# Second layer of a fused attention and MoE kernel as seven products of quarters, with single buffers that make room for it

## Chip, cores, metric

One core of one Trainium2 chip. The metric is the device time of one execution in microseconds. The kernel before takes 723.83 us (median of 3 runs, 723.74 to 724.42).

## The reference, cut

A gated linear attention (4 batches, 8 heads, 768 steps, 48 per head) feeds a two-layer block on 3072 tokens:

```python
def _moe_ref(x, w_in, w_out):      # x 3072x384, w_in 384x2048, w_out 2048x384, all float32
    h = x @ w_in
    g = h * np.cos(h)
    return (g @ w_out).astype(np.float32)
```

The tokens come in 12 groups of 2 x 128 rows; the attention of a group is computed in chunks of 128 steps. The second layer, `g @ w_out`, is what the change rewrites.

## The kernel before: the parts that matter

```python
    def load(g, names, i=None):                       # inputs of group g, on the SP queue
        ...                                           # v has two buffers, the others one
    def g_phase(g, i):                                # "phs": running sum of phases
        matmul(ps, lhsT=turns, rhs=cut(x["tan"], i, 1), start=True, stop=first)
        if not first:                                 # needs tan of the chunk before
            matmul(ps, lhsT=last, rhs=prev, start=False, stop=True)
        ...                                           # ACT casts, VectorE writes tan
    def f_transpose(g, i, n, name):                   # called for kT, then for qT
        tr = ft.tile([C, NB, n * H, 32], F32, tag="tr", name="tr")   # two buffers
        nc.vector.transpose(out=tr, in_=X[g][name[0] + "s"]...)
        moved = rows_d.tile(...)                      # in DRAM
        nc.sync.dma_start(out=moved..., in_=tr)
        # four DMAs DRAM -> kT, or one DRAM -> qT
    def f_scores(n, hh):                              # "sc": reads kT and qT
    def f_xt(g):                                      # yT -> DRAM ("x") -> xT, on the SP queue
    def mm1(g, jp):                                   # "hp": first layer, 6 matmuls of 256 columns
        gate = msb.tile(..., name="gate", bufs=10)
    def mm2(g, i, j0, nj):                            # "op": second layer, 384 columns
        for j in range(j0, j0 + nj):
            matmul(ps, lhsT=gate..., rhs=w_out[:, j], ...)

    def weave(*parts):      # each part: items, from, to; order of the calls = sorted by position
    ...
    for n in range(2, NG):
        weave((logs(n + 1), 0.0, 0.02), (chunks(n), 0.0, 0.36), (second(n - 1, 0), 0.0, 0.38),
              (prods(n + 1), 0.38, 0.39), (each(g_angle, n + 1), 0.39, 0.4),
              (second(n - 1, 1), 0.4, 0.56), (phases(n + 1), 0.49, 0.51),
              (keys(n + 1), 0.52, 0.7), (first(n), 0.56, 1.0), ...)
```

One pass of this loop is a period of about 55 us. The SP queue issues one transfer after the other, so that one that waits holds up all behind it. The order of issue is that of the built program, and not always that of these calls: group 3's `v` is named after `x` and `xT` of group 1, and yet its first load is issued ahead of `x` in the trace below.

## Time and profile before

In the profile's lines PE is TensorE (matrix products), PEld its weight loads, DVE VectorE, ACT and POOL two further engines, SPq the DMA queue of the sync engine. A record is one instruction in the trace; an f32 matmul leaves two.

| | before |
|---|---|
| median of runs | 723.83 us |
| profiled span, granted TensorE clock | 725.1 us, 0.973 |
| TensorE / VectorE / ACT busy | 95% / 55% / 54% |
| second layer of one group | 64 records, 20.65 us |
| start of the first layer (`hp`) of group 1 | 130.8 us |
| mean of eight steady periods (starts of `hp`, groups 2 to 10) | 55.1 us |

### The profile page before, as it was taken

The page shows a single profiled execution, that of the slowest core. Times are in us where ns is not written, and L with a number is a line of the kernel's source. Part 1 is how long each engine was busy: PE and PEld are TensorE (multiplying, and loading weights), DVE is VectorE, ACT ScalarE, POOL GpSimd, SP SyncE. Part 2 cuts the span into 40 slices and gives each one's busy share as a digit, 9 for nine tenths or more (in the row PEclk, how much of TensorE's full clock was granted, in tenths as well). Part 3 has the DMA queues.
Part 4 walks back from the last instruction along what each step waited for, and adds up shares of the span by engine and source line. Part 5 has one row for each costly group of instructions (what it writes and reads, how often), then busy time and mean ns, then how long its engine had stood idle before and what let it go on. Part 6 is the DMA issues. An engine that isn't in the chain of part 4 may idle for free.

```text
span 725.1 us, 9428 instructions
## 1 busy us (share of the span) xinstructions
PE 689.0 (95%) x3574; PEld 523.1 (72%) x3574; DVE 396.3 (55%) x598; ACT 393.3 (54%) x728; POOL 31.4 (4%) x68
## 2 busy tenths in 40 slices
PE   3499799999999999999999999999999999999995
PEld 3397567886886886876776786786786786786773
DVE  4777998553644654655645645645645645731110
ACT  6667796373473484485475475375376376241330
POOL 2001110000000010010010010010010010000000
PEclk9678899999999999999999999999999999999998
DMA  9926726806626566565575575575575482161000
GB/s 269 253 84 156 192 97 130 199 13 141 158 51 146 150 170 131 153 182 130 149 187 128 145 163 120 140 174 123 141 173 122 131 173 69 58 129 55 12 0 28
DMA packets 232115, 94.74 MB, mean 131 GB/s; under 512 B 208366, under 2 KB 220529, under 8 KB 232060
## 3 DMA queue, kind: packets, MB, share of 16 engines
q1 hardware_dynamic: 225324, 68.55, 42.9%
q0 software_dynamic: 6016, 25.17, 10.1%
q8 instruction: 30, 0.49, 0.3%
q10 hardware_dynamic: 720, 0.33, 0.2%
q14 instruction: 25, 0.20, 0.1%
HBM read 69.22 MB, written 24.81 MB: 130 GB/s over the span
## 4 chain that ended last, share of the span: by engine, by line
PE 85%; DMA 6%; DVE 5%; ACT 1%; issue 1%; SPq 1%; POOL 0%; DVEq 0%
PE op L637 33%; PE hp L637 29%; PE sc L637 6%; PE yp L637 5%; PE sp L637 4%; PE phs L637 4%; DMA qT<-moved 2%; PE lgs L637 2%; DMA end<-row 1%; DVE w_out L606 1%; DVE w_out L603 1%; PE yr L637 1%; PE tp L799 1%; DMA raw<-in_moe_w_in_dram 1%; DMA im<-in_a_im_dram 1%
## 5 line engine op out<-in xcount | busy, mean ns | idle before, releaser
L637 PE MATMUL op<-w_out,gate 128*128 128x384 f32 x768 | 262.6, 489 | 0.9 <-DVE w_out L606 0.9
L637 PE MATMUL hp<-xT,w_in 128*128 128x256 f32 x1152 | 255.2, 383 | 0.6 <-ACT xT L860 0.6
L637 PEld LDWEIGHTS hp<-xT,w_in 128*128 128x128 f32 x1152 | 221.8, 193 | 35.0 <-ACT xT L860 1.0
L637 PEld LDWEIGHTS op<-w_out,gate 128*128 128x128 f32 x768 | 142.3, 190 | 95.0 <-issue 3.7
L904 DVE TENSOR_TENSOR gate<-hp,gate 128x512 f32<-128x512 f32 x96 | 65.6, 684 | 135.3 <-ACT gate L653 135.3
L905 ACT ACTIVATE junk<-hp 128x512 bf16<-128x512 f32 x96 | 57.2, 596 | 84.0 <-DVE gate L904 84.0
L653 ACT ACTIVATE gate<-hp,half_pi_b 128x512 f32<-128x512 f32 x96 | 65.7, 684 | 43.2 <-PE hp L637 43.0
L637 PEld LDWEIGHTS sc<-qT,kT 96*128 96x128 f32 x384 | 49.3, 197 | 9.3 <-issue 2.5
L637 PE MATMUL sc<-qT,kT 96*128 96x128 f32 x384 | 50.9, 283 | 1.3 <-DMA qT<-moved 0.9
L818 DVE TENSOR_TENSOR atm<-sc,causal 128x512 f32<-128x512 f32 x48 | 33.0, 687 | 24.7 <-PE sc L637 24.7
L716 DVE SCALAR_TENSOR_TENSOR mag<-Q,lg 128x768 f32<-128x768 f32 (+1 forms) x13 | 11.6, 895 | 63.5 <-ACT Q L653 63.5
L838 ACT COPY yT<-yp 48x512 f32<-48x512 f32 x44 | 25.4, 578 | 38.6 <-PE yp L637 37.9
L748 ACT CAST tan<-phs 128x384 int32<-128x384 f32 x24 | 11.5, 479 | 63.8 <-PE phs L637 63.8
L918 ACT ACTIVATE ot<-op 128x384 f32<-128x384 f32 x24 | 11.6, 482 | 48.6 <-PE op L637 48.6
L652 ACT ACT_TABLE_LOAD x26 | 33.4, 1283 | 0.5
L637 PE MATMUL yp<-atm,v 128*48 128x128 f32 x352 | 33.5, 277 | 0.0
L637 PE MATMUL sp<-v,ks 128*96 128x48 f32 x320 | 29.6, 245 | 0.0
L637 PE MATMUL yp<-qT,state 96*48 96x128 f32 x304 | 29.6, 272 | 0.0
L637 PEld LDWEIGHTS sp<-v,ks 128*96 128x96 f32 x320 | 29.4, 165 | 0.3 <-issue 0.2
L749 DVE TENSOR_TENSOR tan<-phs,tan 128x384 f32<-128x384 f32 x24 | 13.4, 556 | 27.1 <-ACT tan L748 27.0
L617 ACT ACTIVATE e<-e,least_e_b 128x384 f32<-128x384 uint32 (+1 forms) x28 | 18.3, 655 | 16.1 <-DVE e L615 16.0
L637 PE MATMUL lgs<-lg,sums 128*128 128x384 f32 x48 | 19.3, 523 | 7.7 <-DVE lg L690 7.7
(96 smaller groups left out, 695.4 us busy)
## 6 DMA issues: line engine op xcount, KB each, us to landing
moved<-tr SPq DMA_DIRECT2D x20, 768.0 KB
raw<-in_moe_w_in_dram POOLq DMA_DIRECT2D x24, 512.0 KB, 6.1
raw<-in_moe_w_out_dram POOLq DMA_DIRECT2D x32, 384.0 KB, 4.1
kT<-moved SPq DMA_DIRECT2D x40, 192.0 KB
qT<-moved SPq DMA_DIRECT2D x10, 768.0 KB
re<-in_a_re_dram SPq DMA_DIRECT2D x24, 192.0 KB
im<-in_a_im_dram SPq DMA_DIRECT2D x24, 192.0 KB
k<-in_k_dram SPq DMA_DIRECT2D x24, 192.0 KB
```

The costliest lines, as they stand in the source:

```text
L617: nc.scalar.activation(out=e.bitcast(F32), in_=e, func=AF.Relu, scale=-1.0, bias=least_e_b, accum_out=odd[:, ds(next(odds), 1)])
L637: chain(nc.tensor.matmul(out, **kw), "tensor")
L652: chain(nc.scalar.preload_act_table_set(loaded[0]))
L653: chain(nc.scalar.activation(func=func, **kw))
L716: nc.vector.scalar_tensor_tensor(out=u, in0=Q, scalar=HUGE, in1=P, op0=ALU.min, op1=ALU.mult)
L748: nc.scalar.copy(out=ph.bitcast(I32), in_=ps)
L749: nc.vector.tensor_tensor(out=ph, in0=ps, in1=ph.bitcast(I32), op=ALU.subtract)
L818: nc.vector.tensor_tensor(out=y["atm"][:, ts(hh, HH)], in0=ps, in1=causal.unsqueeze(1).to_broadcast([C, HH, C]), op=ALU.mult)
L838: nc.scalar.copy(out=X[g]["yT"][half, :, i], in_=ps[half])
L904: nc.vector.tensor_tensor(out=gate, in0=ps, in1=gate, op=ALU.mult)
L905: nc.scalar.activation(out=junk, in_=ps, func=AF.Square, scale=1.0 / in_scale, accum_out=wide[:, ds(g * (NJ // 2) + jp, 1)])
L918: nc.scalar.mul(out=ot, in_=ps, mul=1.0 / (in_scale * out_scale))
```

## The change

Intent: multiply the 256 x 2048 gates by the 2048 x 384 `w_out` in 2 x 2 quarters with seven products instead of eight (Strassen's method in the form with 15 sums). TensorE does an eighth less in the second layer of 11 groups; VectorE adds the quarters. The sums need room, which is found in buffers.

```diff
-                                     bufs=2 if name == "v" else 1)
+                                     bufs=1)
-    RAW = 6
+    RAW = 4
-        low = stage.tile([C, n], U32, tag="low", name="low")
+        low = stage.tile([C, n], U32, tag="low", name="low", bufs=1)
-            x["cos"], x["sin"] = temp("cos"), temp("sin")
+            x["cos"], x["sin"] = temp("rs"), temp("lg")
-        tr = ft.tile([C, NB, n * H, 32], F32, tag="tr", name="tr")
+        tr = ft.tile([C, NB, n * H, 32], F32, tag="tr", name="tr", bufs=1)
-            X[g]["xT"] = msb.tile([C, ND, G, C], F32, tag="xT", name="xT")
+            X[g]["xT"] = msb.tile([C, ND, G, C], F32, tag="xT", name="xT", bufs=1)
-        gate = msb.tile([C, 2, G * C], F32, tag="gate", name="gate", bufs=10)
+        gate = msb.tile([C, 2, G * C], F32, tag="gate", name="gate", bufs=8)
+    def quarters():      # once: 16 differences of quarters of w_out, into t1, t2, t4 and b12
+    def mixed(g, jp):    # per pair of gate blocks: 4 sums of 256 elements (s1, s2, s3, s4)
+    def seventh(g, p, part):   # half of product p: 4 matmuls of 192 columns
+        ...                    # after the second half: 1 or 2 sums from PSUM into ot
     def first(g):
-        return [lambda jp=jp: mm1(g, jp) for jp in range(NJ // 2)]
+        for jp in range(HJ // 2):
+            yield lambda jp=jp: mm1(g, jp)
+            yield lambda jp=jp: (mm1(g, jp + HJ // 2), mixed(g, jp) if g else None)
     for n in range(2, NG):
-        ... (second(n - 1, 0), 0.0, 0.38), ... (second(n - 1, 1), 0.4, 0.56), ...
+        ... (products(n - 1, 0, 4), 0.0, 0.38), ... (products(n - 1, 4, 7), 0.4, 0.56), ...
```

(Cut: the bodies of the new functions, the same edit for the second `low` and `xT`, and the last pass.)

## The prediction

> **What bounds the kernel now.** I read the page's first part, then the chain that ended last, the groups by form, the waits of TensorE and of the DMA queue, and the timeline of one period. The page and the groups:
>
> ```profile
> PE 689.0 (95%) x3574; PEld 523.1 (72%) x3574; DVE 396.3 (55%) x598; ACT 393.3 (54%) x728; POOL 31.4 (4%) x68
> L637 PE MATMUL op<-w_out,gate 128*128 128x384 f32 x768 | 262.6, 489 | 0.9 <-DVE w_out L606 0.9
> L637 PE MATMUL hp<-xT,w_in 128*128 128x256 f32 x1152 | 255.2, 383 | 0.6 <-ACT xT L860 0.6
> ```
>
> TensorE has work 95% of the time and `op`, the second layer that the change rewrites, is its largest group. Durations there overlap, so I take the pitch from pieces of the chain that ended last (start, us, what):
>
> ```profile
> 45.51 1.79 PE yr L637 x16
> ...
> 676.16 20.72 PE hp L637 x96
> 696.88 20.65 PE op L637 x64
> ```
>
> 384 columns cost 20.65/64 = 322.7 ns, 256 columns 20.72/96 = 215.8 ns, and `yr`, 48 columns behind a load of 128 columns, 112 ns: that is the floor which the weight load sets. The slope is (322.7 - 215.8)/128 = 0.835 ns a column. From 56.6 us on TensorE hardly waits, so its work is the time, unless a wait appears. Where one would appear, the timeline of one period shows (start, us, engine; SPq is the DMA queue):
>
> ```profile
> 397.04 0.81 PE L637 MATMUL phs<-tan,turns 128*128 128x384 f32 x2
> 397.69 0.81 PE L637 MATMUL phs<-tan,last 128*128 128x384 f32 x2
> 398.33 2.74 PE L637 MATMUL op<-w_out,gate 128*128 128x384 f32 x8
> 399.10 0.56 DVE L749 TENSOR_TENSOR tan<-phs,tan 128x384 f32<-128x384 f32 x1 [1.31 <-ACT tan L748]
> 400.91 0.81 PE L637 MATMUL phs<-tan,turns 128*128 128x384 f32 x2
> 401.56 0.81 PE L637 MATMUL phs<-tan,last 128*128 128x384 f32 x2
> 404.78 20.88 PE L637 MATMUL hp<-xT,w_in 128*128 128x256 f32 x96
> 407.86 2.25 DVE L781 STREAM_TRANSPOSE tr<-ks 128x1536 f32<-128x1536 f32 x1
> 410.14 3.06 SPq L784 DMA_DIRECT2D moved<-tr  x2
> 410.61 2.25 DVE L781 STREAM_TRANSPOSE tr<-qs 128x1536 f32<-128x1536 f32 x1
> 413.42 4.64 SPq L787 DMA_DIRECT2D kT<-moved  x4
> 418.17 1.35 SPq L789 DMA_DIRECT2D qT<-moved  x1
> 425.50 1.06 PE L637 MATMUL sc<-qT,kT 96*128 96x128 f32 x8
> ```
>
> Two things to see. An `op` block of 2.6 us stands between the two `phs` blocks, and inside it ACT and VectorE finish `tan` (399.66), which the second block's `last` matmul reads. And keys and queries of the next group run a chain from the second `phs`: products, two transposes into `tr`, out to DRAM, `kT` and `qT` back, just as the 20.7 us of `hp` end. In windows of 1 us the DMA goes quiet at 424.25, 1.25 us before `sc`; in nine steady groups that gap is 1.1 to 1.5 us, and three of them wait there. The chain that ended last goes through this DMA twice:
>
> ```profile
> 308.43 7.99 DMA qT<-moved
> ...
> 363.42 7.12 DMA qT<-moved
> ```
>
> So TensorE is the bound, with this second chain just as long, its slack about zero.
>
> **What the Trainium skill says.** "TensorE: Matmul & The Clock Gate", section "Wait — 56ns, not 53.3ns?": warm spacing is N/2.4 GHz plus about 2.5 ns; "FP8 and Floating Point Precision", section "TensorE Precision Notes": true FP32 takes four passes. The trace has two records per f32 matmul; as two passes each, 384 columns give 2 x 162.5 = 325 ns against 322.7 measured: it agrees. "VectorE: DVE Perf Modes", the section on the TRN2 errata: a fp32 tensor_tensor takes (N+151)/0.96 ns, 691 at 512 and 557 at 384; the trace has about 690 and 550. It agrees, so 256 elements cost 424 ns. "DMA: Bandwidth & Descriptors", section "Anatomy of one DMA": a DMA has about 2 us of fixed cost, most of it the receipt of the last write. The trace agrees in kind: the first `kT` issue, which needs the first `moved`, comes 3.3 us after that one's issue.
>
> **The change, part by part.**
> TensorE: a group's second layer was 2 x 16 matmuls, 64 records, 20.65 us. Seven products of 8 matmuls of 192 columns are 112 records. One costs 215.8 - 64 x 0.835 = 162.4 ns, above the floor of 112, so 18.19 us. Gain 2.46 us, for 11 of 12 groups: **-27.1 us**.
> VectorE, per group: 4 x 4 sums of 256 elements, 16 x 0.42 = 6.8 us; 7 reads of PSUM with 192 elements, about 0.35 each, from 0.55 at 384 (`state<-sp`), 2.5 us. Once: 16 differences of `w_out` of 384 elements, 8.8 us. One period (370.6 to 425.5) has 31.0 us of VectorE; 40.3 in some 53 is 76%. In the `hp` stage 12.1 becomes 19 of 20.7: full, but it holds. ACT loses an evacuation per group.
> Order around `phs`: six half products lie at 0.413 to 0.547 of the period, the `phs` items at 0.495 and 0.505: nothing is between them any more. The first `phs` ends at t, the second's `turns` at t+0.65; `tan` is done at t+1.33 as now (398.33 to 399.66), plus a hop. New wait about 0.8 us in nine groups: **+7 us**.
> `tr` with one buffer: the queries' transpose waits until the keys' `tr` has left, 3.3 us after issue: 413.5 instead of 410.6. It is done at 415.7 at the earliest, later if the new sums go first. If its DMA is issued while `kT` is being issued it costs little; if after all four (418.1), it queues behind their data, which reached to about 421 before and reaches to 420 now. Then 2 us of its own data (768 KB, as from 411 to 413), about 0.5 for the receipt, the issue of `qT` at 422.7, 1.2 to start, 3.3 of data (421 to 424.25 now), 1.1 of receipt: 428.3 against 425.4. In the good case 426.6. I take 2.4 us, nothing hides it, nine groups: **+21 us**.
> Start: first-layer blocks now go 0, 4, 1, 5, so the second needs the third quarter of `w_in`, converted by 64.5 us, while TensorE asks at 59.2. That is 5.3 us of wait, part of it given back in the 4.4 us it waits from 70 to 83 now; fewer buffers for raw words and `low` slow the conversions a little. **+3 us**.
> The rest: differences of `w_out` beside the first `hp` stage, the last sums before product 2 at the end, the guards on one `low`: **+2 us**.
> No cost: one `v`, one `xT` and eight gates come free before their next writer, because `chunks`, `first` and the products run in this order on TensorE; `cos` and `sin` take tiles last read about 5 us before.
> Sum: 723.8 - 27.1 + 7 + 21 + 3 + 2 = 729.7; **729 us**.
>
> **The rivals.**
> 1. The gain arrives: the transposes' chain is hidden, say because the second `moved` slips between the `kT` issues and transfers shrink. Then 723.8 - 27 + 7 + 4 is about 708. For it: TensorE is at 95% and only 0.9 us of waiting for `qT` is on record. Against: the slack is zero in every group, so any delay shows.
> 2. VectorE becomes the bound in the `hp` stage: with 19 of 20.7 us and transposes that sit in its in-order queue until a DMA lands, gates come late, the three PSUM buffers stay full, `hp` itself stops. For: the second gate already comes late behind the transposes (412.77). Against: the later gates have 1.9 us of idle time before each. It would run beside the `qT` delay, not on top; where it is longer than 2.4 us, say 4, the time is about 745.
> 3. Weight loads bound the narrower products: 162 is well above 112 ns, so I give it little; each 10 ns would be 12 us.
>
> **Range and chances.** The gain in matmuls is firm to 1 us, the `phs` wait to 3. The `qT` delay is 1 to 4 us times nine, 9 to 36, the start 0 to 8. So 710 to 747 should hold it 8 times in 10. Faster by over 2% needs less than 709.4, that is nearly hidden transposes: 0.15. Slower needs over 738.3, that is 3.5 us per group or a blocked `hp`: 0.25. Within 2%: 0.60.
>
> **What would show it.** Right: `op` records of about 162 ns pitch, 1232 of them with 192 columns; TensorE waits for `tan` L749 about 0.8 us in nine groups; the queries' transpose starts more than 5 us after the keys' (2.75 now); `sc` waits for `qT` 2 to 3 us in nine groups; TensorE's busy time falls by 27 us while its idle time grows by about 30. Wrong: no wait of `sc` (then 708), waits inside `hp` for gates, or a pitch of `op` near that of 256 columns. I would also be wrong if the program's order on VectorE or the queue is not the one I assume.

("Receipt" in it is the time from the last of a transfer's data to the signal that lets the next step start. The passage that is cut was about DMAs that another engine issues; no term of the sum rests on it.)

## More of the kernel before

The granted clock is the share of TensorE's full clock that the profile shows.

The prediction shows most of the lines of this profile. One more view of the kernel before is needed later: the SP queue around 120 us (start, duration of the issue, engine, line), where the output of the attention goes to DRAM as `x` and comes back as `xT` for the first layer:

```profile
117.64 0.37 SPq L551 DMA_DIRECT2D v<-in_v_dram  x1
118.12 0.38 SPq L722 DMA_DIRECT2D row<-lg  x1
118.59 0.33 SPq L885 DMA_DIRECT2D x<-yT  x1
...
123.58 0.84 SPq L885 DMA_DIRECT2D x<-yT  x1
...
127.05 0.37 SPq L889 DMA_DIRECT2D xT<-x  x1
130.93 0.34 SPq L784 DMA_DIRECT2D moved<-tr  x1
```

`xT` is issued 3.7 us before `hp` of group 1 asks for it, and ahead of the transposed keys.

## The result, and the profile after

The changed kernel takes 760.19 us (median of 4 runs, 755.15 to 762.26), beside 724.12 for the kernel before. The ratio is 1.0476, 95% interval 1.0411 to 1.0541: slower, outside the predicted range. All outputs are right. A ratio here is the mean time of one kernel's runs over that of the other's of the same rounds, so not quite the ratio of the medians that I quote. The profiled runs span 725.1 us before and 753.3 after (it was the fastest of the four runs), and the clock fell from 0.973 to 0.962. What follows explains this profiled run. The other three took 3.5 to 7.1 us longer, at clocks of 0.951 to 0.958. By their spans these clocks mean some 6 to 17 us more at half clock, so 3 to 9 us of work (an estimate): enough for the difference, but no trace of them was kept.

TensorE's busy time and the pitch of the products, from the page and the chain that ended last of the changed kernel:

```profile
PE 679.1 (90%) x4102; PEld 596.9 (79%) x4102; DVE 494.5 (66%) x867; ACT 390.0 (52%) x717; POOL 33.3 (4%) x68
...
363.17 2.60 PE op L637 x16
```

16 records in 2.60 us are 162.5 ns each: the work saved is there. Yet TensorE's busy time falls by 9.9 us only, and its idle time grows. TensorE's waits of the changed kernel (us in total, times, longest):

```profile
PE sc L637 <- DMA qT<-moved: 22.0, 7, 3.6
PE phs L637 <- DVE tan L749: 8.6, 10, 3.6
...
PE sc L637 <- issue: 6.0, 2, 3.0
PE hp L637 <- DMA xT<-x: 5.4, 1, 5.4
```

In nine groups the scores wait 2.8 to 3.6 us, 28.0 us in all, where the kernel before had 0.9 + 0.3. The timeline of one period of the changed kernel shows how it comes about:

```profile
362.26 0.91 PE L637 MATMUL phs<-tan,last 128*128 128x384 f32 x2 [0.52 <-DVE tan L749]
...
368.93 2.24 DVE L781 STREAM_TRANSPOSE tr<-ks 128x1536 f32<-128x1536 f32 x1
371.20 0.33 SPq L784 DMA_DIRECT2D moved<-tr  x1
374.65 3.88 SPq L787 DMA_DIRECT2D kT<-moved  x4
374.91 2.24 DVE L781 STREAM_TRANSPOSE tr<-qs 128x1536 f32<-128x1536 f32 x1
378.62 1.45 SPq L784 DMA_DIRECT2D moved<-tr  x1
384.02 0.33 SPq L789 DMA_DIRECT2D qT<-moved  x1
389.62 1.13 PE L637 MATMUL sc<-qT,kT 96*128 96x128 f32 x8 [3.13 <-DMA qT<-moved]
```

The queries' transpose starts 5.98 us after the keys' (2.75 before): it needs `tr`, which is still leaving. The keys' `moved` has landed at 374.65, when `kT` is issued; so the four `kT` issues fill the queue until 378.53, and the queries' `moved`, ready at 377.15, goes out at 378.62, behind all of `kT`'s data. The chain that ended last gives it 5.3 us from issue to landing, where the keys' took 3.4 (371.20 to 374.65), and `qT` another 5.5:

```profile
378.62 5.34 DMA moved<-tr
384.02 5.46 DMA qT<-moved
```

Something else I had not counted at all shows in stretches of 4 us around the wait of two groups of the changed kernel (stretch, then its length; busy time and records of PE, PEld, DVE, ACT, POOL; granted clock, DMA share, GB/s):

```profile
268.00:272.00 4.00, 1.00 (x5) 0.54 (x3) 2.17 (x6) 3.52 (x8) 1.25 (x3) 1.00 0.66 179
272.00:276.00 4.00, 3.91 (x16) 3.94 (x17) 2.16 (x5) 3.68 (x5) 1.22 (x3) 0.57 0.86 281
386.00:390.00 4.00, 0.87 (x6) 0.50 (x5) 2.62 (x6) 3.47 (x7) 1.94 (x5) 1.00 0.73 181
390.00:394.00 4.00, 4.00 (x31) 4.00 (x30) 2.27 (x4) 3.79 (x6) 0.53 (x2) 1.00 0.94 325
```

After the wait that ends at 272.1 us the clock is halved: 16 records in 4 us instead of 31. After the like wait that ends at 389.6 it isn't. Adding up, in slices of 1 us, TensorE's busy time times (1 - granted clock), the work lost to half clock after 165 us is 10.7 us (0 before).

Last, the wait for `xT`, once, in group 1. The SP queue of the changed kernel there:

```profile
117.93 0.99 SPq L551 DMA_DIRECT2D v<-in_v_dram  x2
...
124.01 1.53 SPq L885 DMA_DIRECT2D x<-yT  x2
131.44 0.34 SPq L784 DMA_DIRECT2D moved<-tr  x1
131.90 0.38 SPq L889 DMA_DIRECT2D xT<-x  x1
```

With one buffer the loads of group 2's `v` wait for the matmuls that read group 1's. That alone is not what delays `x`: in the kernel before a load of group 3's `v` stood ahead of `x` too, and left at about the same time (117.64, here 117.93). But the order of the queue has changed. The first `x` now stands behind the loads of `k` and `q` (124.01, not 118.59). The second, which `xT` needs as well, leaves 1.5 us later (at 125.1, not 123.58). And `xT` now stands behind `moved`, which waits for the transpose on VectorE; in the kernel before it stood ahead of it. Had it left as long after the second `x` as before (3.47 us), it would have gone at 128.6, an estimate; it goes at 131.90. `hp` waits 5.43 us, and its 96 records then take 23.83 us instead of 20.88, at half clock from 135.6 to 142.4: 2.9 us of work lost.

### The profile page after: what moved, and what is told of

Same layout as the page of the kernel before. It is cut to its first block, busy times and chain, and to the rows that moved or that the text cites. A ratio compares the mean times of both kernels' runs of the same rounds, so it can differ in the third digit from the quotient of the medians.

```text
span 753.3 us, 10785 instructions
## 1 busy us (share of the span) xinstructions
PE 679.1 (90%) x4102; PEld 596.9 (79%) x4102; DVE 494.5 (66%) x867; ACT 390.0 (52%) x717; POOL 33.3 (4%) x68
## 4 chain that ended last, share of the span: by engine, by line
PE 69%; DMA 14%; DVE 9%; ACT 3%; issue 3%; SPq 0%; ACTq 0%; POOL 0%; DVEq 0%; POOLq 0%
PE op L637 24%; PE hp L637 23%; PE sc L637 7%; PE yp L637 5%; DMA qT<-moved 5%; PE sp L637 3%; PE phs L637 3%; DMA moved<-tr 3%; PE lgs L637 2%; DMA raw<-in_moe_w_out_dram 2%; DVE tr L781 1%; DVE tan L749 1%; DVE gate L904 1%; DMA line_d<-even 1%; DMA raw<-in_moe_w_in_dram 1%
## 5 line engine op out<-in xcount | busy, mean ns | idle before, releaser
L637 PE MATMUL op<-w_out,gate 128*128 128x192 f32 (+1 forms) x592 | 124.5, 359 | 4.3 <-DVE w_out L606 4.3
L637 PEld LDWEIGHTS op<-w_out,gate 128*128 128x128 f32 x592 | 101.7, 199 | 15.8 <-DVE w_out L606 8.0
L637 PE MATMUL sc<-qT,kT 96*128 96x128 f32 x384 | 57.6, 299 | 28.7 <-DMA qT<-moved 22.0
L637 PEld LDWEIGHTS sc<-qT,kT 96*128 96x128 f32 x384 | 53.0, 210 | 34.3 <-issue 25.7
L972 DVE SCALAR_TENSOR_TENSOR ot<-op,ot 128x192 f32<-128x192 f32 x77 | 26.2, 352 | 68.7 <-PE op L637 68.5
L637 PE MATMUL op<-t,s 128*128 128x192 f32 x352 | 63.3, 329 | 0.0
L637 PEld LDWEIGHTS op<-t,s 128*128 128x128 f32 x352 | 57.3, 190 | 2.8 <-issue 0.4
L748 ACT CAST tan<-phs 128x384 int32<-128x384 f32 x24 | 11.5, 478 | 50.1 <-PE phs L637 50.1
L637 PEld LDWEIGHTS op<-w_out,s 128*128 128x128 f32 x176 | 29.1, 190 | 2.4
L637 PE MATMUL op<-t,gate 128*128 128x192 f32 x176 | 30.5, 327 | 0.1
L637 PE MATMUL op<-w_out,s 128*128 128x192 f32 x176 | 30.4, 326 | 0.0
L637 PE MATMUL sp<-v,ks 128*96 128x48 f32 x320 | 29.6, 245 | 0.0
```

Source lines behind the costliest of these rows:

```text
L637: chain(nc.tensor.matmul(out, **kw), "tensor")
L748: nc.scalar.copy(out=ph.bitcast(I32), in_=ps)
L972: nc.vector.scalar_tensor_tensor(out=out_, in0=x["op"], scalar=scale, in1=known, op0=ALU.mult, op1=ALU.add)
```

## Experiments

**Theories.** Mine after reading the traces: (A) the single `tr` delays the queries, about 27 us of waits before `sc`; (B) those waits halve the clock behind them, about 11 us; (C) the single `v` delays `xT`, about 8 us with its clock drop. Rivals: the other savings (raw words, `low`, `xT`, gates, shared tiles) carry the loss; or VectorE, 66% busy with the sums, holds the transposes up, so that the seven products themselves carry it. Eleven kernels were run, in three batches, each beside runs of the kernel before on the same chip (medians 728.03, 726.77 and 723.88).

### 1. Only the single `tr`, on the kernel before

```diff
-        tr = ft.tile([C, NB, n * H, 32], F32, tag="tr", name="tr")
+        tr = ft.tile([C, NB, n * H, 32], F32, tag="tr", name="tr", bufs=1)
```

> The kernel before with nothing changed but one buffer for tr. Theory A (the single tr delays the queries' transpose and with it qT, TensorE then idles 3 us before sc in nine groups, and some of these idle stretches drop the granted clock): sc waits for qT 2.5 to 3.5 us in nine groups, the granted clock falls below 0.97, time 750 to 765. Rival B (the extra VectorE work of the seven products is what delays the chain, one tr costs little by itself): waits under 1 us, time 724 to 733.

Measured: 773.61 us, ratio 1.0644 (1.0585 to 1.0702). This is above the 750 to 765 expected. Its profiled run spans 770.0 us, 44.9 more than before:

```profile
PE sc L637 <- DMA qT<-moved: 21.4, 7, 3.6
PE sc L637 <- issue: 8.1, 2, 4.5
```

The scores wait 29.5 us (1.2 before), and 14.2 us of work are lost to half clock: 42.5 of the 44.9. This one buffer alone costs more than the whole change did, with no seven products and no sums on VectorE in the program. That speaks against the rival of the fuller VectorE.

### 2. and 3. The change with two `tr`, and its control

Two buffers for `tr` don't fit beside everything else: the second came out of the raw words (`RAW = 3`). So a control with that alone was run.

```diff
# seven_tr2
-    RAW = 4
+    RAW = 3
-        tr = ft.tile([C, NB, n * H, 32], F32, tag="tr", name="tr", bufs=1)
+        tr = ft.tile([C, NB, n * H, 32], F32, tag="tr", name="tr", bufs=2)
# seven_raw3: the first edit alone
```

> The changed kernel with two tr buffers again, paid for with 3 instead of 4 raw buffers. Theory A: the waits of sc for qT shrink to under 1 us, the clock comes back to 0.97, time 705 to 718 (724 - 27 for the products, + 5 for the phs wait, + 3 to 12 for the start). Rival B: qT still comes 2 to 3 us late because VectorE is full, time 740 to 760.

> Control for seven_tr2: the changed kernel with 3 raw buffers and still one tr. Both theories: within 6 us of the changed kernel, 750 to 768, with the same waits of sc.

Measured: 727.46 us with two `tr`, ratio 1.0004 (0.9962 to 1.0046); 770.51 us for the control, ratio 1.0602. The first lies between the two ranges expected, the second just above its own. So the second `tr` takes 43 us off, and the loss of one raw buffer puts some 10 us on. Of the 11.5 us between the profiled spans of the control and the change, 4.5 are the start (`hp` of group 1 at 141.12, not 136.65 us), and 4.9 are half clock (15.6 us after 165 us, not 10.7) after waits that are hardly longer (29.7 us, not 28.0). With two `tr` `hp` of group 1 starts at 142.40 us, the waits before `sc` sum to 4.6 us, and the mean of the steady periods is 54.1 us, below the 55.1 of the kernel before: that is where the seven products are seen for the first time.

### 4. The change with two `tr`, without touching the raw words

The queries' transpose writes to the space of the logarithms and reciprocals, which are dead by then. This takes no room.

```diff
+    def pair(name):      # lg and rs side by side in one tile of the tag "pair"
+            x["lg"], x["rs"] = pair("pair")
-            x["cos"], x["sin"] = temp("rs"), temp("lg")
+            x["sin"], x["cos"] = pair("pair")
-        tr = ft.tile([C, NB, n * H, 32], F32, tag="tr", name="tr", bufs=1)
+        if name == "kT":
+            tr = ft.tile([C, NB, n * H, 32], F32, tag="tr", name="tr", bufs=1)
+        else:
+            tr = gt.tile([C, 2 * G * DM], F32, tag="pair", name="tr").rearrange(...)
```

> The change as it is, but the queries' transpose writes into the space of the tiles that hold the logarithms and reciprocals (dead by then), so the queries no longer wait for the keys' tile to leave; no buffer count of the weight stage is touched, unlike in seven_tr2. My theory: the single tr carries the 28 us of waits before sc and the clock drops after them (about 12 us over the periods), so 760 - 40 = 720 us, range 714 to 727; the wait of 5.4 us for xT and the drop behind it (8.5 us) and the nine waits for tan (5 us) stay. Waits before sc under 8 us in sum, clock at or above 0.972. Rival: the waits come from VectorE being fuller with the sums, so a second tr moves little: sc still waits 2 us or more in most groups and the time stays above 740.

Measured: 719.41 us, ratio 0.9933 (0.99 to 0.9967), where 720 was expected; clock 0.978. TensorE waits 2.8 us before `sc` and loses nothing to half clock after 165 us. The waits for `xT` and `tan` stay, as expected. One period of it, on VectorE, the queue and TensorE:

```profile
357.33 2.25 DVE L790 STREAM_TRANSPOSE tr<-ks 128x1536 f32<-128x1536 f32 x1
359.61 3.09 SPq L793 DMA_DIRECT2D moved<-tr  x2
360.07 2.27 DVE L790 STREAM_TRANSPOSE tr<-qs 128x1536 f32<-128x1536 f32 x1
...
375.31 1.13 PE L637 MATMUL sc<-qT,kT 96*128 96x128 f32 x8 [0.42 <-DMA qT<-moved]
```

The queries follow 2.74 us behind the keys again. The same sums stand on VectorE as in the change, so the fuller VectorE isn't what held the transposes up.

### 5. The change with dummy work in the wait

12 matmuls on constants go ahead of the first `sc` of a group. Nothing needed comes earlier; TensorE only idles less.

```diff
+                if n == g * G and hh == 0 and g > 2:
+                    yield lambda: (busy(12), f_scores(g * G, 0))
```

> The changed kernel with 12 matmuls of no use (24 records of some 110 ns, 2.7 us) put on TensorE just before the first sc of groups 3 to 11, where it idles about 3 us. Nothing that the result needs comes earlier. Theory C (the idle stretch lowers the granted clock for a while after it, worth some 12 us in all): the record after the stretch keeps its 110 ns pitch in all groups, clock 0.97 or more, time 10 to 16 us below the changed kernel. Rival D (the waits alone make the loss, the slower sc is only a late start): no gain, time equal to the changed kernel or up to 5 us above.

Measured: 751.7 us, ratio 1.0323 (1.0277 to 1.037), against 1.0476 for the change: work that is good for nothing makes the kernel some 10 us faster, the low end of what was expected.

```profile
PE sc L637 <- DMA qT<-moved: 7.1, 7, 2.3
...
PE sc L637 <- issue: 1.3, 2, 0.7
```

The clock is 0.975 and the work lost to half clock after 165 us is 1.6 us, in the one group that still waited over 2 us. So the clock, theory B, is a cost of its own beside the waits.

### 6. The seven-product order: product 0 ahead of the scores

```diff
-        ... (products(n - 1, 0, 4), 0.0, 0.38), ...
+        ... (products(n - 1, 0, 4), -0.08, 0.38), ...
```

> The changed kernel with one tr, but the first product (2.6 us of TensorE work that needs no qT) issued before the first sc of each group instead of after it. Theory A: the delay of qT stays, but 2.6 of the 3.1 us of waiting are filled with useful work and the clock stays up: 9 x 2.5 + 12 = 35 us below the changed kernel, 720 to 732, ratio to before 0.995 to 1.015. Rival: products wait for the last sums, or the chain starts 2.6 us later as well, and little is won.

Measured: 723.59 us, ratio 0.9952 (0.9908 to 0.9995).

```profile
PE sc L637 <- DMA qT<-moved: 5.0, 7, 1.1
...
PE sc L637 <- issue: 1.0, 2, 0.7
```

The queries come no earlier, but 2.6 us of useful matmuls fill the wait: the waits before `sc` fall from 28.0 to 6.0 us and none of them is over 1.1 us, and no work is lost to half clock after 165 us. 22.0 + 10.7 = 32.7 us would be gained; the profiled spans differ by 31.3.

### 7. The other savings alone, on the kernel before

One `v`, one `xT`, one `low`, `RAW = 4`, eight gates, `cos` and `sin` in the tiles `rs` and `lg`; `tr` keeps two buffers and there are no seven products. The edit is the buffer part of the diff above without its `tr` line.

> The kernel before with every other saving of the change (one v, one xT, one low, 4 raw buffers, 8 gates, cos and sin in the tiles of rs and lg) but two tr and no seven products. My prediction held these to be free. Theory A: 724 to 736; the only new wait is that of the first hp block of group 1 for xT (5 us and some 3 us of lowered clock after it), if the one v is what moves xT back in the DMA queue. Rival: the other single buffers also cost in every group, over 740.

Measured: 735.35 us, ratio 1.0108 (1.0067 to 1.0149). These savings aren't free as the prediction had it. TensorE's waits of this kernel, and the stretch that follows the wait:

```profile
PE hp L637 <- DMA xT<-x: 5.4, 1, 5.4
...
136.00:143.00 7.00, 5.65 (x13) 4.50 (x14) 0.00 (x0) 0.12 (x1) 0.00 (x0) 0.51 1.12 188
```

5.4 us of waiting and 2.8 us of work lost to half clock (5.65 us of work at 0.51) are 8.2 of the 9.5 us between the profiled spans (734.6 and 725.1). Another 1.2 us stand before this wait: `hp` of group 1 asks at 132.0, not 130.8. What remains for the others of these buffers is within the noise.

### 8. The change with the loads of `v` named after `xT`

```diff
         yield lambda: f_xt(g)
-        if g + 2 < NG:
-            yield lambda: load(g + 2, ("v",))
+        if g + 1 < NG:
+            yield lambda: load(g + 1, ("v",))
```

(and the two early loads of the start moved likewise).

> The changed kernel with the loads of v named after the transfers of x and xT in the program, one group later each. Theory: the early-named load of v, which has to wait for its only buffer, pushes x and xT back in the DMA queue in group 1; the wait of hp for xT (5.4 us) goes, and with it the lowered clock after it (3 us): 6 to 10 us below the changed kernel, ratio to the kernel before about 1.035. Rival: xT stays behind moved, no change.

Measured: 761.35 us, ratio 1.0454 (1.0405 to 1.0504): no gain. The wait for `xT` is indeed gone: `xT` leaves at 130.80, ahead of `moved` (134.66), though it has one buffer as in the change, and `hp` of group 1 takes 20.88 us again. It starts at 134.26, only 2.4 us earlier than in the change, because the start before it is some 3 us longer here (the load of `v` behind group 1's matmuls leaves at 121.15, not 117.93); why was not taken apart. The 5.3 us won by the end of this stage were given back later: the scores wait 29.6 us, and now all nine waits are followed by half clock, with 20.4 us of work lost after 165 us (10.7 in the change). Why nine instead of five, the next part answers.

### What decides whether the clock drops

The traces of the runs above hold enough for it. I took the granted clock in slices of 0.2 us around every wait of TensorE of 1 us or more, and from it the start and the end of each drop. For the changed kernel (us; the last column is worked out below):

```
work starts  idle before  half clock          idle in one slot
136.65       5.43         135.61 to 142.43    3.41
215.48       2.92         none                1.55
272.09       3.09         272.14 to 275.55    3.09
331.53       3.38         330.16 to 336.99    2.01
389.62       3.13         none                1.70
445.95       2.81         446.22 to 449.63    2.81
505.00       2.98         504.24 to 511.07    2.22
563.84       3.58         none                2.01
620.44       3.05         620.30 to 623.71    2.91
679.47       3.04         none                1.89
```

In each trace all drops start a whole number of 3.413 us apart, within 0.02 us, and after 100 us they last 3.41 or 6.82 us, one or two such slots (three or four at the start of the program). So the core judges TensorE in slots of 3.413 us that run on whatever the program does. The Trainium skill, "TensorE: Matmul & The Clock Gate", section "What's actually happening", states just that: a free-running window of 3413 ns, and half clock after an idle one. The table agrees, and adds that the slot need not be idle throughout. With the grid laid by the drops of each trace, the last column is the most of the idle stretch that falls into one slot. Over the changed kernel and experiments 1, 3, 5 and 8, 37 waits of 2 us or more lie after 165 us. 29 of them were followed by a drop, and each of these has 1.97 us or more in one slot; the 8 others have 2.01 us or less. A wait of 3 us then costs 3 us, or 3 plus 1.7 to 3.4 (half of one or two slots, an estimate), as it happens to lie in the grid. How many drops a run gets is in this sense luck: five of nine in the change, seven in its control of experiment 3. In `seven_xt` all nine lay badly (2.09 us or more). I found this rule in the traces and didn't test it with a kernel built for it.

### 9. to 11. Everything together, and two parts taken out again

`best` is the change with the queries' `tr` in "pair" (4), product 0 first (6), the loads of `v` late (8), two `low` buffers again, group 0's first-layer blocks in the old order, and the `phs` items spread so that products lie between them:

```diff
-              (products(n - 1, 4, 7), 0.4, 0.56), (phases(n + 1), 0.49, 0.51),
+              (products(n - 1, 4, 7), 0.4, 0.56), (phases(n + 1), 0.4675, 0.5175),
```

`best_noorder` is that without product 0 first, `best_nophs` without the spread `phs`.

> The changed kernel with the queries' tr in the space of rs and lg (no more memory), two low buffers, the first-layer blocks of group 0 in the old order, the loads of v named later, half a product between the two phs blocks, and the first product before sc. Theory A: no wait of sc, phs or xT left, 700 to 708, ratio 0.97 or below (27 us of products less a few). Rival: some of the waits have other causes, above 712.

> The best kernel without moving product 0 ahead of the scores. My theory: with two places for tr the chain of the transposes ends when TensorE asks, as in the kernel before, so the order buys only the last bit: 696 to 702 us, waits before sc of 0 to 0.8 us a group and no clock drop. Rival: the order is what carries the gain (it took 36 us off the change alone), so that without it waits of 2 us and more come back and the time is above 715.

> The best kernel with the phs items where the change has them, nothing between the two blocks. My theory: nine waits for tan of 0.52 to 0.57 us come back, 5 us, so 701 us (699 to 704). Rival: the chain from the second phs to the scores only starts later in the period by moving a block between, so the 5 us were given back there and the time is 696 as it is.

Measured: 696.3 us for `best` (695.95 to 697.44), ratio 0.9578 (0.9538 to 0.9618): faster than both kernels, and than the 700 to 708 expected. 702.06 us, ratio 0.9702, without product 0 first; 702.07 us, ratio 0.97, without the spread `phs`. The page of `best`:

```profile
PE 661.4 (95%) x4102; PEld 586.5 (84%) x4102; DVE 487.3 (70%) x867; ACT 383.1 (55%) x717; POOL 33.1 (5%) x68
```

TensorE's busy time is 27.6 us below that of the kernel before, and 95% of the span is busy as before. That this equals the predicted 27 is in part luck: 1.7 us of it lie before `hp` of group 1, where no product of the seven runs yet; from there on it is 25.9 us. No wait of `sc` or `hp` over 0.7 us is left, and of the steady waits for `tan` three of 0.18 us. Without product 0 first, `sc` waits for 3.2 us in all and no clock drop comes back: with two places for `tr` the order buys little, and the rival that it carries the gain falls. Its time was at the edge of what I expected. The last two kernels ran on another chip than `best`, so the 6 us between them are known to a few us only. Without the spread `phs` the nine waits for `tan` are back (8.9 us in all against 4.5): 4.4 of the 6.0 us by which the way from `hp` of group 1 to that of group 11 is longer (526.7 and 520.6 us). So this wait was on the path, and shifting one block removes it without giving it back. `best` also reaches `hp` of group 1 at 126.4 us instead of 136.65; beyond the 5.4 of `xT` that is 4.8 us of the start, which I didn't take apart into its causes.

## Why the prediction was wrong

By its own steps, on the profiled runs (+28.2 us):

| step | predicted | measured |
|---|---|---|
| seven products | -27.1 | about -27 (162.5 ns a record; 2.43 to 2.46 us a group) |
| nothing between the `phs` blocks | +7 | +5.0 (0.52 to 0.57 us, nine times) |
| single `tr` | +21 (2.4 nine times) | +26.8 (2.8 to 3.6 nine times) |
| half clock after these waits | not seen | +10.7 |
| one `v`, one `xT` | 0 | +5.4, and 2.9 of half clock |
| start | +3 | +0.4 up to the wait for `xT` |
| not assigned | +2 | about +4 |

Right: the bound, the gain on TensorE, the sums' cost on VectorE (0.42 us each as taken) and that VectorE would not become the bound: no gate holds `hp` up in the table of waits. Rival 1, hidden transposes, and rival 3, the weight loads, did not come. The chain that would grow was named rightly, with its cause, its nine groups and its sign; experiments 1 and 4 show it.

Wrong in size, the `tr` step: I worked out a good case of 1.2 us and a bad one of 2.9 us, and took 2.4 between them. But the order of the queue decides between the two: `kT` is always issued before the queries' transpose ends (374.65 against 377.15), so the bad case comes, and the queries' own `moved` behind `kT`'s data took 5.3 us to land. In all nine groups `moved` of the queries went out after the last `kT`. The bad case times nine is 26; 26.8 was measured.

Wrong, the step that a wait of n us costs n us. TensorE without work can also be TensorE at half speed afterwards. The Trainium skill says so on the page I had cited for the pitch ("TensorE: Matmul & The Clock Gate", section "Why this matters for your kernels": "No PE-idle gaps >~3µs between matmul bursts"), and I put waits of about that length into the sum without asking what follows them. The runs show 10.7 us for it in the change, 14.2 in experiment 1 and 20.4 in experiment 8; experiment 5 shows it apart from the waits.

Wrong, the step "No cost: one `v`". I asked only when the buffer comes free for its own next writer. But with the single buffer the order of the queue changed: `x`, which the first layer needs, is issued later, and `xT` stands behind `moved`. The prediction had named this danger in its last sentence (an order of the queue other than the one assumed) without a cost for it. Experiment 7 shows 8.2 us for these buffers together, experiment 8 that the place of `v`'s load decides, since there the wait is gone with one `v` and one `xT`. How the built program gets its order was not looked into.

Without the two omitted costs (10.7 + 8.3) the measured change would have been 28.2 - 19.0 = +9.2 us, against +5.9 in the prediction's sum: the `tr` step alone, mis-sized by 6, would not have left the range. What stays open: the 4 us not assigned, the 5 us between the profiled run and the median of the four, and what each buffer of the weights' stage costs at the start.

## What to carry to other kernels

A saving on the engine that bounds is only worth what the buffers paid for it leave: before giving up a second buffer, follow its chain to the end and see which transfer it puts behind which, and look again at the order in which each queue issues, which a smaller buffer can change. Where a change makes TensorE wait 2 us or more again and again, add the half clock to the sum, and put useful matmuls into the wait if the wait itself can't be removed. And look for room in tiles that are dead at that moment before taking it from ones that overlap transfers.

## What the Trainium skill lacked or had wrong

- "TensorE: Matmul & The Clock Gate", section "Why this matters for your kernels": the limit of about 3 us of idle time is too loose here. Seven waits of 2.33 to 2.98 us halved the clock, and one of 3.58 us did not; in these traces what counts is some 2.0 us of idle time within one slot of 3.413 us, and each drop after a wait lasts one or two slots (3.41 or 6.82 us). The page doesn't state how much idle time within a window is enough.
- No page gives the time from issue to landing of a transfer that stands behind others on the same queue ("DMA: Bandwidth & Descriptors" would be its place). Here a 768 KB transfer issued on the SP queue right behind four of 192 KB took 5.3 us, where one issued with nothing just ahead of it took 3.4 us.
